# Attention and expert layers in one TensorE stream: how the second group's K reaches its scores, and where two pieces of work are put in the order of issue

## The chip, the core and the metric

The kernel runs on one core of a Trainium2 chip. The metric is the time of one execution in microseconds of the device; lower is better. Engines are named as in the profile: PE (TensorE, matrix products; PEld its weight loads), DVE (VectorE), ACT (ScalarE), POOL (GpSimd), SP (SyncE, which here only issues transfers).

## The reference

Two stages. A linear attention with a complex decay per head and channel, step by step over 768 positions, and a dense layer of four experts on its output.

```python
for t in range(S):                      # S = 768; B, H, D = 4, 8, 48
    new_re = ar * S_re - ai * S_im      # ar, ai: normalised decay of step t
    new_im = ar * S_im + ai * S_re
    S_re, S_im = new_re + einsum('bhd,bhe->bhde', k[:, :, t], v[:, :, t]), new_im
    y[:, :, t] = einsum('bhd,bhde->bhe', q[:, :, t], S_re)
x = y.transpose(0, 2, 1, 3).reshape(3072, 384)
for e in range(4):
    out += p[:, e:e + 1] * (relu(x @ w1[e]) @ w2[e])    # w1[e]: 384 x 1024, w2[e]: 1024 x 384
```

## The kernel before

Products of the expert layers are made in about single precision from parts: each operand is split into a high part and a remainder (hi and lo for weights, xh and xl for x, hh and hl for the hidden values), and three of the four partial products are added up.

The 3072 positions are worked in twelve groups g of 256, counted here from 0, each of two chunks c of 128. For each group three things happen.

**Preparation**, mostly on DVE and ACT. norm scales the decays. prefix forms running products of the decays: steps inside segments of eight (tiles pf), a tree over the segments (sk), and then the four long products and two sums that carry the tree's results to all positions (tile fm; cmul, line 373). finish gives, with q and k, the tiles Q and K: head makes Q, tail makes K. A group's Q and K are laid out by rows of heads, 128 partitions; the scores want them in another layout, 112 partitions by head, in the tiles Qst and Kst.

**Attention** on PE. There are two ways into Qst and Kst. send (line 548) issues ten transfers for one chunk, or for both: five row blocks for the real and five for the imaginary part. With short=True the four blocks of 16 rows are issued from POOL, the other six from SP; otherwise all ten from SP. The other way is over PE: turned (turn0, turn1 for the chunks) transposes K into KT with positions on the partitions (tile ktp), ACT copies it, and turned_back (back0, back1) transposes KT back per head (tile kp, line 601), and ACT copies that to Kst (line 602). KT is needed in any case, by increment (inc0, inc1; tile dp), which forms K times V for the running state Gs. The scores (sc0, sc1; tile sc) multiply Kst with Qst, DVE masks them into scs, values (val0, val1; tile yp) multiplies them with v and adds Qst times the state. ACT copies the result to y. rotate brings the state to the next group's start with the factors of t_factors. Groups 0 and 1 (g < NSEL = 2) go by near_attention, all others by attention. For groups 0 to 2 (g < XSEL = 3), y is turned into x on PE (turn_x, tile xp); from group 3 on, y is stored to memory (y_d) and read back (xa), which all groups store anyway for the second phase. split_x makes xh on ACT and xl on DVE.

**Block** g, the first two experts for the group's x: eight steps of W1 (w1_step, tile ph, 18 products) and W2 (w2_step, tile po, 12 products), W2 one step behind. W1 needs xh of both chunks for its first products, xl for the last three of each half.

The loop over g from 1 on issues block g - 1 (moe1) and, ahead of its step k, calls between(k). There, at step first = FIRST[g] and the steps up to end, one piece of group g's attention is issued (the generator near_attention or attention, cut by its yields), and at the end its x is split. advance issues preparation of the groups to come by planned costs: each yield in norm, prefix and front gives a cost in microseconds, and each step k spends a budget (STEP plus MORE). The scheduler then orders each engine's instructions by a simulated timeline; so what is issued later can run earlier where it is ready. Two helpers bind it: keep_in_program_order keeps an instruction where it was issued, behind(a, b) puts a after b on one engine. wts["w1"] is the first product of the second half of the newest W1 step.

In the second phase, from about 560 us on, the other two experts are worked with a scheme of fewer products; the change doesn't touch it.

For group 1 before the change: Q's first chunk and then its second are sent; K's first chunk goes through turn0 and back0; the third piece (store_y, t_factors, inc1, rotate) is issued at step 7 of block 0.

Of the kernel before, what the change touches and what calls it, by code (L numbers as in the profile page):

```python
# [11 lines left out]
ALU = mybir.AluOpType  # L12
# [23 lines left out]
SEG = 8  # L36
# [21 lines left out]
NSEL = 2  # L58
XSEL = 3
# [66 lines left out]
def fast_path(ctx, tc, qkP, aP, vP, probsP, w, out, flag):  # L126
    nc = tc.nc
# [38 lines left out]
    wts = {}  # L166
# [62 lines left out]
    def split_x(g, parts):  # L229
        xh = moe.tile([P, NJ, G], F32R, tag="xh", name=f"xha{g}")  # L230
        xl = moe.tile([P, NJ, G], F32R, tag="xl", name=f"xla{g}")
        for ts, x in parts:
            ins = nc.scalar.activation(xh[:, :, ts], x, AF.Copy)  # L233
            tc.keep_in_program_order(ins)
            tc.keep_in_program_order(nc.vector.tensor_tensor(xl[:, :, ts], x, xh[:, :, ts], op=ALU.subtract))  # L235
        wts["x"] = ins
        return xh, xl

# [59 lines left out]
    with ExitStack() as c1:  # L298
# [74 lines left out]
        def cmul(x, br, bi, shape, nm):  # L373
            n = 1
            for d in shape:
                n *= d
            names = ["x", "y", "z"][:len(shape)]
            pat = "p c (" + " ".join(names) + ") -> p c " + " ".join(names)
            kw = dict(zip(names, shape))
            half = NJ * G // 2  # L380
            if n <= half:
                t = tmp(f"{nm}a")
                v1, v2 = (t[:, :, k * half:k * half + n].rearrange(pat, **kw) for k in range(2))
            else:
                v1, v2 = (tmp(f"{nm}{k}")[:, :, :n].rearrange(pat, **kw) for k in "ab")
            if len(shape) < 3:
                nc.vector.tensor_tensor(v1, x, bc2(br), op=ALU.mult)
                nc.vector.tensor_tensor(v2, x, bc2(bi), op=ALU.mult)
            else:
                nc.vector.tensor_tensor(v1[:, 0], x[:, 0], br, op=ALU.mult)  # L390
                nc.vector.tensor_tensor(v2[:, 1], x[:, 1], bi, op=ALU.mult)
                nc.vector.tensor_tensor(v1[:, 1], x[:, 1], br, op=ALU.mult)
                nc.vector.tensor_tensor(v2[:, 0], x[:, 0], bi, op=ALU.mult)
            nc.vector.tensor_tensor(x[:, 0], v1[:, 0], v2[:, 1], op=ALU.subtract)
            nc.vector.tensor_tensor(x[:, 1], v1[:, 1], v2[:, 0], op=ALU.add)

        last = {}

# [42 lines left out]
        def prefix(g, A, cuts=(1, NS)):  # L441
            for i in range(1, SEG):
                x = A[:, :, i, :]
                z = tmp(f"pf{g}_{i}").rearrange("p c n -> p (c n)")[:, :4 * MS].rearrange(
                    "p (c d m) -> p c d m", c=2, d=2)
                nc.vector.tensor_tensor(z, x.unsqueeze(2).broadcast_to([P, 2, 2, MS]), bc2(A[:, :, i - 1, :]),  # L446
                                        op=ALU.mult)
                nc.vector.tensor_tensor(x[:, 0], z[:, 0, 0], z[:, 1, 1], op=ALU.subtract)
                nc.vector.tensor_tensor(x[:, 1], z[:, 1, 0], z[:, 0, 1], op=ALU.add)
                yield 1.07  # L450
            Al = A[:, :, SEG - 1, :]
            As = A.rearrange("p c i (j s) -> p c i j s", j=NJ)
            k = 1
            for lo, hi in zip(cuts, cuts[1:]):
                while k < hi:
                    nb = MS // (2 * k)
                    Ak = Al.rearrange("p c (b s) -> p c b s", s=2 * k)
                    br, bi = (Ak[:, c, :, k - 1:k].broadcast_to([P, nb, k]) for c in range(2))
                    cmul(Ak[:, :, :, k:], br, bi, [nb, k], f"sk{g}_{k}")
                    yield 0.9  # L460
                    k *= 2
                shape = [SEG - 1, NJ, hi - lo]
                br, bi = (As[:, c, SEG - 1:, :, lo - 1:hi - 1].broadcast_to([P] + shape) for c in range(2))
                cmul(As[:, :, :SEG - 1, :, lo:hi], br, bi, shape, f"fm{g}_{lo}")
                yield 0

        def pick(g, nm, X, dst, s, w):
# [102 lines left out]
        def chunk(g, c, K, y):  # L570
# [34 lines left out]
            def increment(joined=False):  # L605
                if last:
                    return
                d_ps = ps_a.tile([M, H, D], F32, tag="pa", name=f"dp{g}_{c}")
                for h in range(H):
                    for o, n in ((0, IM), (IM, D)):  # L610
                        ins = nc.tensor.matmul(d_ps[o:o + n, h, :], KT[:, c, h, o:o + n], vc[:, h * D:(h + 1) * D],  # L611
                                               start=True, stop=True)
                        if joined or h or o:
                            tc.keep_in_program_order(ins)
                        if g == 0 and c == 1 and h == 0 and o == 0:
                            behind(ins, wts["w1"])
                Gt = Gs[c]
                if first:
                    nc.scalar.activation(Gt, d_ps, AF.Copy, scale=-1.0)
                else:  # L620
                    nc.vector.tensor_tensor(Gt, state[g, c], d_ps, op=ALU.subtract)
                state[g, c + 1] = Gt
# [89 lines left out]
        def near_attention(g, QK):  # L712
            Q, K = QK
            y = small.tile([M, HP, G], F32, tag="y", name=f"y{g}", bufs=1)
            (turn0, back0, inc0, sc0, val0), (turn1, back1, inc1, sc1, val1) = (chunk(g, c, K, y) for c in range(CG))
            if g == 0:
                turn_over(WARM[1], pick(g, "q", Q, Qst, 0, C))
                yield
                turn0(parts=(0,))
                yield  # L720
                turn_over(WARM[2], turn0(last["act"], parts=(1,)))
                back0()
                state["norm"] = norm(1, A[1], prev=(state["kt", 0, 0], last["dve"], state["kst", 0, 0]))
                next(state["norm"])
                sc0((0,))
                sc0((1,), turn1(prev_pe=state["sc"]))
                inc0()
                yield send(Q, Qst, 1, short=True)
            else:
                yield send(Q, Qst, 0, 1)  # L730
                yield send(Q, Qst, 1)
                turn0()
                back0()
                inc0()
                sc0()
                yield
                turn1()
            back1()
            sc1()
            val0()  # L740
            val1()
            xs = [turn_x(g, c, y) for c in range(CG)]
            yield xs
            store_y(g, y)
            t_factors(g)
            inc1()
            rotate(g)
# [90 lines left out]

        def front(g, A, qk):
            pre = prefix(g, A, cuts if g < NSEL else (1, NS))  # L840
            Q, K, head, tail = finish(g, A, qk)

            def ahead():
                for r in pre:
                    if r == 0:
                        return
                    yield r

            if g < NSEL:
                pieces = near_attention(g, (Q, K))  # L850
                yield from ahead()
                yield 1.8
                head(0, 1)
                yield 1.6
                next(pieces)
                if g == 0:
                    tail(0, 1)
                    next(pieces)
                yield from ahead()
                yield 2.0  # L860
                last["act"] = head(1, CG)
                yield 1.6
                if g > 0:
                    last["q"] = next(pieces)
                    tail(0, 1)
                    yield 2.7
                last["dve"] = tail(1, CG)
                if g == 0:
                    last["q"] = next(pieces)
                yield 2.7  # L870
                todo[g] = pieces
                return
            yield from ahead()
            yield 3.9
            last["act"] = head(0, CG)
            yield 3.0
            yield None
            send(Q, Qst, short=True)
            last["dve"] = tail(0, CG)
            yield 4.8  # L880
            last["q"] = send(K[0], Kst, short=True)
            todo[g] = attention(g, (Q, K))
# [53 lines left out]
        for g in range(1, NG + 1):  # L936
            if g == NG:
                check_all()
            first = FIRST.get(g, 3)
            end = first + (2 if g < NSEL else 1)  # L940

            def between(k, g=g, first=first, end=end):
                if k in LATE.get(g, ()) and NG - 1 in todo:
                    next(late, None)
                if g == 1 and k == 1:
                    for _ in todo.pop(0):
                        pass
                if g == 1 and k > 0:
                    for i in range(NPRE + EARLY + 2 * k - 2, min(NPRE + EARLY + 2 * k, NF1)):
# [594 lines left out]
```

## Time and profile before

| | us |
|---|---|
| median of 3 runs | 960.18 |
| lowest and highest run | 959.71, 960.25 |
| the profiled execution, its own time | 960.0 |
| its span, first to last instruction | 958.2 |
| PE busy in it | 933.9 |
| DVE busy | 745.2 |
| ACT busy | 483.0 |
| POOL busy | 210.7 |

The profile shows one execution. Times in its rows count from the start of the span; busy time is the time in which an engine had an instruction at work. A time in brackets behind an instruction is how long its engine stood idle ahead of it, with what ended that. The granted clock of TensorE is 1.00 of full speed in all the windows read here.

### The profile page before, as it was taken

To read this page: it belongs to the slowest core of one execution; us is meant where nothing else is said; L and a number is where in the kernel's file an instruction comes from. 1 tells how busy PE (TensorE), PEld (TensorE's weight loads), DVE (VectorE), ACT (ScalarE), POOL (GpSimd) and SP (SyncE) were. 2 spreads that over 40 slices of the span, in tenths; PEclk is the share of its full clock that TensorE was granted. 3 is DMA by queue.
4 is the path that set the end of the run, shared out by engine and by line. 5 is a ranking of instruction groups with operands and counts; after the bars stand their busy time and mean duration, and the time that the engine had idled before them with its cause. 6 is when DMAs were issued, how large, how long until landed. Compare 5 with 4: busy or idle time off the path is not lost.

```text
span 958.2 us, 19409 instructions
## 1 busy us (share of the span) xinstructions
PE 933.9 (97%) x7388; PEld 908.3 (95%) x7388; DVE 745.2 (78%) x1630; ACT 483.0 (50%) x1030; POOL 210.7 (22%) x294
## 2 busy tenths in 40 slices
PE   5999999999999999999999999999999999999997
PEld 3899999999999999999999999999999999999997
DVE  7898989989989999888996577748485757666642
ACT  7766446363564736547343555635454554444430
POOL 6030111020211202111111036333424352322000
PEclk9999999999999999999999999999999999999999
DMA  9585264544535546353437799131514433131112
GB/s 314 171 172 139 60 159 89 150 99 142 149 96 129 129 138 156 117 135 109 117 109 226 269 316 275 50 121 38 148 57 144 162 85 102 50 99 51 50 50 78
DMA packets 75029, 125.73 MB, mean 131 GB/s; under 512 B 9600, under 2 KB 50224, under 8 KB 74928
## 3 DMA queue, kind: packets, MB, share of 16 engines
q1 hardware_dynamic: 60464, 94.69, 32.7%
q0 software_dynamic: 14464, 29.72, 13.3%
q8 instruction: 60, 0.98, 0.5%
q14 instruction: 41, 0.34, 0.1%
HBM read 75.94 MB, written 31.46 MB: 112 GB/s over the span
## 4 chain that ended last, share of the span: by engine, by line
PE 89%; DVE 6%; DMA 3%; ACT 2%; issue 1%; SPq 0%; ACTq 0%; DVEq 0%
PE ph L246 21%; PE pob L995 20%; PE po L267 19%; PE pb L995 17%; PE sc L635 3%; PE yp L667 2%; PE dp L611 2%; PE yp L677 2%; PE ktp L584 1%; DMA RX<-w 1%; PE sc L652 1%; DMA shi<-late_d 1%; DVE pf L446 1%; PE xp L706 1%; DVE xl L1001 0%
## 5 line engine op out<-in xcount | busy, mean ns | idle before, releaser
L995 PE MATMUL pob<-shi,hid 128*128 128x384 f32 x528 | 148.5, 335 | 0.5 <-DVE hid L1004 0.5
L267 PE MATMUL po<-whi,hh 128*128 128x384 f32 x384 | 129.7, 338 | 0.0
L267 PE MATMUL po<-wlo,hh 128*128 128x384 f32 x384 | 128.9, 336 | 0.0
L257 ACT ACTIVATE hh<-ph 128x512 fp32r<-128x512 f32 x96 | 57.2, 596 | 121.8 <-PE ph L246 117.5
L1007 POOL TENSOR_TENSOR Z<-Z 128x384 f32<-128x384 f32 x84 | 89.9, 1104 | 114.6 <-DMA Z<-y_d 57.0
L246 PE MATMUL ph<-xha,whi 128*128 128x256 f32 x576 | 103.8, 287 | 1.3 <-ACT xha L233 1.3
L246 PE MATMUL ph<-xla,whi 128*128 128x256 f32 x576 | 101.0, 283 | 2.0 <-DVE xla L235 2.0
L246 PE MATMUL ph<-xha,wlo 128*128 128x256 f32 x576 | 102.0, 284 | 0.0
L995 PE MATMUL pb<-xh,shi 128*128 128x384 f32 x291 | 97.1, 335 | 1.0 <-DVE pb L1001 1.0
L995 PEld LDWEIGHTS pob<-shi,hid 128*128 128x128 f32 x528 | 96.4, 188 | 1.2 <-DVE hid L1004 1.1
L995 PE MATMUL pb<-xl,shi 128*128 128x384 f32 x288 | 96.2, 334 | 0.0
L995 PE MATMUL pb<-xh,slo 128*128 128x384 f32 x288 | 96.2, 334 | 0.0
L246 PEld LDWEIGHTS ph<-xha,whi 128*128 128x128 f32 x576 | 85.9, 190 | 5.3 <-issue 2.4
L258 DVE SCALAR_TENSOR_TENSOR hl<-ph,hh 128x512 fp32r<-128x512 f32 x96 | 65.9, 687 | 31.0 <-ACT hh L257 30.3
L995 PE MATMUL pob<-slo,hid 128*128 128x384 f32 x264 | 88.2, 334 | 0.0
L267 PE MATMUL po<-whi,hl 128*128 128x384 f32 x384 | 85.2, 338 | 0.5 <-DVE hl L258 0.5
L246 PEld LDWEIGHTS ph<-xla,whi 128*128 128x128 f32 x576 | 82.8, 191 | 2.7 <-DVE xla L235 2.4
L246 PEld LDWEIGHTS ph<-xha,wlo 128*128 128x128 f32 x576 | 82.8, 190 | 0.4
L998 ACT ACTIVATE SN<-pb 128x384 f32<-128x384 f32 x96 | 47.4, 494 | 66.7 <-PE pb L995 59.4
L1001 DVE TENSOR_TENSOR xl<-Z,xh 128x384 fp32r<-128x384 f32 x104 | 59.2, 598 | 21.7 <-ACT xh L998 16.3
L998 ACT ACTIVATE hid<-pb 128x384 fp32r<-128x384 f32 x76 | 37.3, 491 | 71.9 <-PE pb L995 71.5
L267 PEld LDWEIGHTS po<-whi,hh 128*128 128x128 f32 x384 | 72.4, 189 | 0.3 <-ACT acc L775 0.2
(238 smaller groups left out, 2119.4 us busy)
## 6 DMA issues: line engine op xcount, KB each, us to landing
qk<-qkP SPq DMA_DIRECT2D x24, 384.0 KB, 4.0
acc_d<-acc POOLq DMA_DIRECT2D x24, 384.0 KB, 5.3
ACC<-acc_d SPq DMA_DIRECT2D x48, 192.0 KB, 3.2
A<-aP SPq DMA_DIRECT2D x22, 384.0 KB, 6.1
v<-vP SPq DMA_DIRECT2D x24, 288.0 KB, 3.0
Z<-y_d SPq DMA_DIRECT2D x16, 384.0 KB, 4.8
Qst<-Q SPq DMA_DIRECT2D x40, 145.1 KB, 3.9
Kst<-K SPq DMA_DIRECT2D x40, 144.0 KB, 3.8
```

What stands on the lines that cost most here:

```text
L246: ins = nc.tensor.matmul(ph[:, u, :], wt[:, j * P:(j + 1) * P], xt[:, j, :], start=(n == 0), stop=(n == 3 * NJ - 1))
L257: wts["hh"] = nc.scalar.activation(hh, ph, AF.Relu)
L258: nc.vector.scalar_tensor_tensor(hl, ph, 0.0, hh, op0=ALU.max, op1=ALU.subtract)
L267: nc.tensor.matmul(po[t], part[0][:, u, t * P:(t + 1) * P], wts[i][n][:, HD:], start=(i % FE == 0 and part[0] is hh and n == 0), stop=(i % ...
L611: ins = nc.tensor.matmul(d_ps[o:o + n, h, :], KT[:, c, h, o:o + n], vc[:, h * D:(h + 1) * D], start=True, stop=True)
L635: ins = nc.tensor.matmul(to, k, q, start=True, stop=True)
L667: ins = nc.tensor.matmul(yo, vc[:, vo:vo + n], scs[2 * c + h // 4][:, h % 4, :], start=True, stop=first)
L677: ins = nc.tensor.matmul(yo, st[:, o:o + n], Qc[:, o // D, :], start=False, stop=True)
L995: return tc.keep_in_program_order(nc.tensor.matmul(*args, **kw))
L998: return pin(nc.scalar.activation(dst, src, fn, scale=scale))
L1001: pin(nc.vector.tensor_tensor(dst, x, y, op=op))
L1007: nc.gpsimd.tensor_tensor(dst, x, y, op=op)
```

## The change

It has three parts.

- Group 1, first chunk of K: sent to Kst by transfers (six on SP, four on POOL) instead of turned back on PE (back0 falls away; turn0 stays for the increment). tail(0, 1), which makes that chunk, is issued ahead of the sends; the second chunk of Q is sent behind K's, and its small blocks are issued from POOL.
- Group 1, the last piece (store_y, t_factors, inc1, rotate): issued at step 1 of block 1, behind its first W1 step, as group 0's already was in block 0, and the increment of chunk 1 is put behind wts["w1"]. The attention's pieces thus take two steps of the block, not three.
- Group 3's prefix: the first long product of fm is put behind the last product of xl of the split issued before it (wts["xl"]), on DVE. cmul returns its first instruction for that.

```diff
--- before.py
+++ after.py
@@ -232,7 +232,8 @@
         for ts, x in parts:
             ins = nc.scalar.activation(xh[:, :, ts], x, AF.Copy)
             tc.keep_in_program_order(ins)
-            tc.keep_in_program_order(nc.vector.tensor_tensor(xl[:, :, ts], x, xh[:, :, ts], op=ALU.subtract))
+            wts["xl"] = nc.vector.tensor_tensor(xl[:, :, ts], x, xh[:, :, ts], op=ALU.subtract)
+            tc.keep_in_program_order(wts["xl"])
         wts["x"] = ins
         return xh, xl
 
@@ -384,15 +385,16 @@
             else:
                 v1, v2 = (tmp(f"{nm}{k}")[:, :, :n].rearrange(pat, **kw) for k in "ab")
             if len(shape) < 3:
-                nc.vector.tensor_tensor(v1, x, bc2(br), op=ALU.mult)
+                ins = nc.vector.tensor_tensor(v1, x, bc2(br), op=ALU.mult)
                 nc.vector.tensor_tensor(v2, x, bc2(bi), op=ALU.mult)
             else:
-                nc.vector.tensor_tensor(v1[:, 0], x[:, 0], br, op=ALU.mult)
+                ins = nc.vector.tensor_tensor(v1[:, 0], x[:, 0], br, op=ALU.mult)
                 nc.vector.tensor_tensor(v2[:, 1], x[:, 1], bi, op=ALU.mult)
                 nc.vector.tensor_tensor(v1[:, 1], x[:, 1], br, op=ALU.mult)
                 nc.vector.tensor_tensor(v2[:, 0], x[:, 0], bi, op=ALU.mult)
             nc.vector.tensor_tensor(x[:, 0], v1[:, 0], v2[:, 1], op=ALU.subtract)
             nc.vector.tensor_tensor(x[:, 1], v1[:, 1], v2[:, 0], op=ALU.add)
+            return ins
 
         last = {}
 
@@ -461,7 +463,9 @@
                     k *= 2
                 shape = [SEG - 1, NJ, hi - lo]
                 br, bi = (As[:, c, SEG - 1:, :, lo - 1:hi - 1].broadcast_to([P] + shape) for c in range(2))
-                cmul(As[:, :, :SEG - 1, :, lo:hi], br, bi, shape, f"fm{g}_{lo}")
+                full = cmul(As[:, :, :SEG - 1, :, lo:hi], br, bi, shape, f"fm{g}_{lo}")
+                if g == XSEL:
+                    behind(full, wts["xl"])
                 yield 0
 
         def pick(g, nm, X, dst, s, w):
@@ -612,7 +616,7 @@
                                                start=True, stop=True)
                         if joined or h or o:
                             tc.keep_in_program_order(ins)
-                        if g == 0 and c == 1 and h == 0 and o == 0:
+                        if g < NSEL and c == 1 and h == 0 and o == 0:
                             behind(ins, wts["w1"])
                 Gt = Gs[c]
                 if first:
@@ -728,9 +732,9 @@
                 yield send(Q, Qst, 1, short=True)
             else:
                 yield send(Q, Qst, 0, 1)
-                yield send(Q, Qst, 1)
+                yield send(K[0], Kst, 0, 1, short=True)
+                yield send(Q, Qst, 1, short=True)
                 turn0()
-                back0()
                 inc0()
                 sc0()
                 yield
@@ -861,8 +865,9 @@
                 last["act"] = head(1, CG)
                 yield 1.6
                 if g > 0:
+                    tail(0, 1)
+                    next(pieces)
                     last["q"] = next(pieces)
-                    tail(0, 1)
                     yield 2.7
                 last["dve"] = tail(1, CG)
                 if g == 0:
@@ -937,13 +942,13 @@
             if g == NG:
                 check_all()
             first = FIRST.get(g, 3)
-            end = first + (2 if g < NSEL else 1)
+            end = first + 1
 
             def between(k, g=g, first=first, end=end):
                 if k in LATE.get(g, ()) and NG - 1 in todo:
                     next(late, None)
-                if g == 1 and k == 1:
-                    for _ in todo.pop(0):
+                if g <= NSEL and k == 1:
+                    for _ in todo.pop(g - 1):
                         pass
                 if g == 1 and k > 0:
                     for i in range(NPRE + EARLY + 2 * k - 2, min(NPRE + EARLY + 2 * k, NF1)):
```

## Rows read from the trace of the kernel before

**Rows 1.** The page, parts 1 and 4: busy time of PE; the chain by engine.
```profile
PE 933.9 (97%) x7388; PEld 908.3 (95%) x7388; DVE 745.2 (78%) x1630; ACT 483.0 (50%) x1030; POOL 210.7 (22%) x294
...
PE 89%; DVE 6%; DMA 3%; ACT 2%; issue 1%; SPq 0%; ACTq 0%; DVEq 0%
```

**Rows 2.** Waits of PE, 60 to 200 us: total, times, longest.
```profile
PE ph L246 <- DVE xla L235: 2.0, 1, 2.0
PE kp L601 <- ACT KT L588: 0.7, 1, 0.7
PE ph L246 <- ACT xha L233: 0.7, 1, 0.7
```

**Rows 3.** Windows: busy time and instructions by engine (PE, PEld, DVE, ACT, POOL), clock, DMA.
```profile
103.00:149.00 46.00, 46.00 (x435) 44.74 (x432) 41.46 (x102) 18.88 (x39) 4.50 (x9) 1.00 0.41 107
...
153.00:195.00 42.00, 41.32 (x405) 39.21 (x405) 38.32 (x86) 21.59 (x47) 4.45 (x9) 1.00 0.48 125
195.00:240.00 45.00, 45.00 (x450) 43.88 (x450) 40.48 (x89) 23.68 (x51) 5.39 (x10) 1.00 0.45 120
```

**Rows 4.** Chain that ended last, in order of time, 84 to 156: start, length, what.
```profile
86.69 0.66 PE kp L601 x6
...
87.58 0.36 PE kp L601 x2
...
88.90 1.98 PE sc L652 x16
...
102.15 1.06 PE dp L611 x30
```

**Rows 5.** Timeline of DVE and ACT, 78 to 90: start, length, instruction.
```profile
78.89 1.02 DVE L543 TENSOR_TENSOR K<-A,u 128x384 f32<-128x384 f32 x2
...
88.05 1.08 ACT L602 ACTIVATE Kst<-kp 112x512 f32<-112x512 f32 x2
```

**Rows 6.** Timeline of SP and POOL: transfers issued, groups 1 and 3.
```profile
88.71 0.83 SPq L367 DMA_DIRECT2D qk<-qkP  x2
...
165.58 3.68 SPq L553 DMA_DIRECT2D Kst<-K  x6
165.84 1.43 POOL L553 DMA_DIRECT2D Kst<-K  x3 [5.44 <-DVE K L543]
...
171.42 0.83 SPq L367 DMA_DIRECT2D qk<-qkP  x2
```

**Rows 7.** DMA issues: count, KB each, median us from issue to landing.
```profile
Kst<-K POOLq DMA_DIRECT2D x40, 16.0 KB, 3.3
...
Qst<-Q SPq DMA_DIRECT2D x8, 72.6 KB, 2.2
...
Qst<-Q SPq DMA_DIRECT2D x4, 72.0 KB, 4.6
```

**Rows 8.** Timeline of ACT, DVE and PE: second halves of two splits; fm and K of group 3.
```profile
102.19 0.49 ACT L233 ACTIVATE xha<-xp 128x384 fp32r<-128x384 f32 x1 [0.85 <-PE xp L706]
...
148.70 0.49 ACT L233 ACTIVATE xha<-xp 128x384 fp32r<-128x384 f32 x1 [2.44 <-PE xp L706]
...
149.34 0.83 DVE L390 TENSOR_TENSOR fm_1a<-A 128x651 f32<-128x651 f32 x1
...
152.93 0.62 PE L246 MATMUL ph<-xla,whi 128*128 128x256 f32 x3 [1.99 <-DVE xla L235]
...
164.60 1.82 DVE L543 TENSOR_TENSOR K<-A,u 128x768 f32<-128x768 f32 x2
```

**Rows 9.** Timeline of PE, start of block 0.
```profile
50.56 0.62 PE L246 MATMUL ph<-xha,whi 128*128 128x256 f32 x3 [0.58 <-ACT xha L233]
```

**Rows 10.** Timeline of PE, first scores of group 3.
```profile
172.52 0.43 PE L635 MATMUL sc<-Qst,Kst 112*64 112x128 f32 x2
```

**Rows 11.** Timeline of ACT and PE, start of block 4.
```profile
238.35 0.85 ACT L233 ACTIVATE xha<-xa 128x768 fp32r<-128x768 f32 x1 [0.53 <-DMA xa<-y_d]
...
239.26 0.61 PE L246 MATMUL ph<-xha,whi 128*128 128x256 f32 x3
```

## The prediction

> **What bounds the kernel now.** I read the page first: TensorE (PE) is busy in 97% of the span, and the chain that ended last is PE in 89% of its length, DVE in 6% [rows 1]. So the end moves by what PE is spared, products or waits, and by little else. The list of PE's waits between 60 and 200 us comes next; three are over half a microsecond, 3.4 us in all [rows 2]. The windows show where PE stands still: not between 103 and 149, 0.68 us between 153 and 195, not after that [rows 3]; the wait for xla falls just after 149 [rows 8]. The same rows show where the danger is: DVE is busy in 41.46 of the 46 us before 149 and in 38.32 of the 42 after 153 (91%). It is a second bound close under PE, and where PE gets ahead, DVE's results may not be there yet.
>
> **First part: K's first chunk by transfers.** Removed in group 1: eight transposes on PE (kp, line 601) and two copies on ScalarE (ACT, line 602). In the chain the transposes alone are 0.66 + 0.36 = 1.02 us; from their first to the scores it is 88.90 - 86.69 = 2.21 us, in which the increment lies too, and undivided that lasts 1.06, so 1.15 at most [rows 4]. I take 1.1. The two copies, 1.08 us of ACT [rows 5], bring nothing beyond it: the scores that waited for them are freed by the transfers instead, and ACT is no bound.
>
> Added: ten transfers of K, six on SP's queue and four on POOL's; four of Q's second chunk go from SP to POOL. DVE has K's first chunk at 78.89 + 1.02 = 79.9, its first half some 0.5 us sooner, at 79.4 [rows 5]. Six such issues take SP 3.68 us in group 3 [rows 6], so the last goes out by 83.1; the large sends of a second chunk, at this place of the group, landed in 2.2 us [rows 7]: K is there at 85.3. On POOL three issues take 1.43 us [rows 6], so four take 1.9, and with 3.3 us to landing [rows 7] it is 79.9 + 5.2 = 85.1. The first scores move from 88.9 to 87.8: 2.5 us of room. The bound from above is the 4.6 us that the large sends of Q's first chunk took under the weights' loads [rows 7]: 87.7, still in time. So no wait. Behind these sends on SP stand the second chunk of Q, and the loads of the next qk and A, which wait for Q's last send and go out at 88.71 [rows 6]. Then: 83.1 + 3.7 = 86.8 for six of Q, plus 2.2, is 89.0, 0.3 us later; A of group 3 and qk of group 2 are read tens of microseconds afterwards. Cost nothing.
>
> The Trainium skill ("DMA: Bandwidth & Descriptors", Rules for kernel authors) speaks against this part: small transfers should be coalesced, and under 64 KB one pays mostly overhead. With that page's fixed 2.0 us and 436 GB/s a send of 72 KB takes an estimated 2.2 us, and the 2.2 of the trace agrees; by rule or by row K lands at 85.3 and the sum is the same, since the overhead lies on queues that are idle here.
>
> The wait of 0.7 us for KT in the same attention [rows 2] belongs to the second chunk, which stays as it is: no gain. Should W2 products of the block come to lie there, 0.7 more is saved; that is the bound from below.
>
> **Second part: last increment behind the next W1.** Store, factors, increment and rotation of group 1 are issued after the first W1 step of block 1. Now the increment fills the 1.06 us between the turning of x and W1 (102.15 to 103.21) [rows 4], while ACT ends the second half of xh at 102.19 + 0.49 = 102.68 [rows 8]. Group 0 shows the place without it: there the increment already lies inside W1, and PE waits 0.58 us for xh [rows 9]. So W1 starts some 0.45 us earlier and pays the 1.06 a little later: a loss of 0.6. From below zero, if W2 products of the last step fill the hole; from above 1.06, if nothing of W1 moves up. The increment's readers on DVE, a difference and four products of the rotation, come later by about 2 us, and who waits for them is the state of group 2, tens of microseconds on; SP's store of y is read in the second phase only. Cost nothing. The 0.5 us of planned budget that goes with the third piece shifts preparation by no more than that.
>
> **Third part: the fourth prefix behind the third x's split.** DVE starts the four long products (fm) of group 3 at 149.34, one every 0.75 us, ahead of the second half of xl of group 2, though ACT has its input ready at 148.70 + 0.49 = 149.19; PE reaches xl, waits 1.99 us and goes on at 152.93 [rows 8]. With the order turned xl runs from about 149.4 to 150.0. PE's products that need only xh last until 152.93 - 1.99 = 150.94, so the wait goes whole: 2.0. DVE pays nothing, for xl lies ahead of fm's closing sums in either order. Bounds: 2.0, or zero if the pin turns out empty because the prefix is issued against an earlier split.
>
> **What is late next.** By now PE is 1.1 - 0.6 + 2.0 = 2.5 us ahead and would reach the scores of group 3, now at 172.52 [rows 10], at 170.0. They read the K that DVE finishes at 164.60 + 1.82 = 166.42 [rows 8], and the load that waits for K's last send goes out at 171.42 [rows 6]: K is in place 1.1 us before it is read now, and 1.4 us too late for a PE that is 2.5 ahead. DVE can gain a little where it waits for PE, and W1 and W2 products can step in while the scores wait; but PE already waits 0.7 us for the x that comes out of this attention [rows 2], so what the scores lose is not all made good. I take 0.5 us back; bounds 0 and 1.4.
>
> **Sum**, against the profiled execution's own 960.0 us (span 958.2): 960.0 - 1.1 + 0.6 - 2.0 + 0.5 = 958.0. That execution is 0.2 us under the median of the runs, 960.18, within their spread. A change of under 0.2%, 1.9 us, can hardly be told from none with this kernel.
>
> **Rivals.**
> 1. DVE and the transfers take most back. K of group 3 does not come earlier, PE's lead shrinks to its 1.1 us of room, and x of group 4 has hardly any room either: ACT ends its xh at 238.35 + 0.85 = 239.20, W1 starts at 239.26 [rows 11]. Time 960.0 - 1.1 = 958.9, between 958.3 and 960.2. For it: DVE's 91%. Against: DVE has 4.5 idle us of 45 after 195 [rows 3], enough to catch up. The case of an empty pin ends here too: 960.0 - 1.1 + 0.6 = 959.5.
> 2. Slower: K's first chunk lands late. PE runs in the order written, so scores that stand ahead of their K stop all behind them, one for one from 87.8 on. It decides from 90.3, where the 2.5 us are eaten up; from 92.2 on the kernel is 0.2% slower. Landing at 92.7 would give 960.0 + 0.6 - 2.0 + 4.9 - 1.1 = 962.4. For it: 4.6 us to landing under load, and ten sends in place of eight transposes. Against: even those 4.6 end at 87.7, and no wait of PE for a K that was sent stands in its list. The rule of the Trainium skill on small transfers, named above, would point this way.
> 3. Better: W2 products fill the 0.7 us of the attention's wait and the hole of 0.6, and K of group 3 keeps up: 960.0 - 1.1 - 0.7 - 2.0 = 956.2.
>
> **Chances.** The forecast, with its own range of 957.0 to 958.26: 0.42. Better: 0.12. DVE takes it back: 0.34. Slower: 0.12, a sixth of it with a loss under 0.2%. Faster by over 0.2% (under 958.26) is then 0.54, within 0.2% 0.36, slower 0.10. The range of 956.2 to 961.0 leaves out the far end of the better case and most of the slower one.
>
> **What would show it.** Right: no kp products in group 1, its first scores about 1.1 us earlier and without a wait for Kst; PE waiting about 0.6 us for xha ahead of block 1; no wait for xla at block 2; the scores of group 3 near 170.5. Wrong: a wait of PE for sent K near 88 us; a wait for xha ahead of block 3 that has grown from 0.7 us by what was saved before; waits at later blocks, where there are none now.

## The result, and the profile after

The changed kernel is slower: 965.91 us in the median of 6 runs (964.48 to 967.23), against 960.21 (959.47 to 961.91, 6 runs) for the kernel before on the same chip. The ratio is 1.0059, with a 95% interval of 1.0046 to 1.0072. The profiled execution took 966.38 us with a span of 964.7, 6.5 us more than the span before.

All three edits are to be seen where they were meant to act. The loss comes behind them. The third part binds only the product that cmul returns, so one of the four long products still runs ahead of xl (149.00), then xl (149.76), then the other three; that is enough to take PE's wait away. First, PE's waits between 60 and 200 us in the changed kernel (total, times, longest; [rows 2] is the same list before):

```profile
PE ph L247 <- ACT xha L233: 4.0, 2, 3.4
PE kp L605 <- ACT KT L592: 1.2, 1, 1.2
```

The wait of 2.0 us for xla is gone. The wait for xha, one of 0.7 before, is now two: 0.58 ahead of block 1 and 3.40 ahead of block 3. The wait for KT has grown by half a microsecond. Between 200 and 560 us, where the kernel before waits for nothing that its list names, there are two more:

```profile
PE sc L639 <- DMA Kst<-K: 0.9, 1, 0.9
PE po L268 <- ACT acc L779: 0.9, 1, 0.9
```

The windows of the changed kernel show the same by place (length, then busy time of PE, PEld, DVE, ACT and POOL with their instructions, granted clock, DMA share, GB/s):

```profile
0.00:60.00 60.00, 46.62 (x377) 38.57 (x378) 48.83 (x130) 43.19 (x89) 23.67 (x42) 1.00 0.73 223
60.00:103.00 43.00, 40.95 (x356) 39.41 (x355) 38.82 (x101) 24.47 (x53) 11.03 (x19) 1.00 0.72 167
...
149.00:153.00 4.00, 4.00 (x34) 4.00 (x33) 3.97 (x7) 1.48 (x3) 0.91 (x1) 1.00 0.14 16
...
194.00:196.00 2.00, 0.00 (x0) 0.00 (x0) 1.06 (x2) 0.00 (x0) 0.00 (x0) 1.00 0.55 185
196.00:198.00 2.00, 1.05 (x5) 1.05 (x6) 1.07 (x2) 0.84 (x1) 0.00 (x0) 0.77 0.00 0
198.00:200.00 2.00, 2.00 (x9) 2.00 (x9) 1.39 (x2) 0.49 (x2) 0.00 (x0) 0.50 0.00 0
...
200.00:300.00 100.00, 98.26 (x923) 95.56 (x922) 87.87 (x187) 53.98 (x108) 15.52 (x29) 1.00 0.50 123
```

Four of the same windows of the kernel before:

```profile
0.00:60.00 60.00, 47.58 (x377) 39.01 (x378) 48.73 (x130) 43.39 (x89) 23.65 (x42) 1.00 0.73 223
60.00:103.00 43.00, 42.06 (x392) 40.62 (x390) 38.56 (x101) 25.44 (x55) 7.07 (x11) 1.00 0.68 157
...
149.00:153.00 4.00, 2.02 (x16) 1.61 (x14) 3.97 (x9) 1.25 (x3) 0.91 (x1) 1.00 0.29 35
...
200.00:300.00 100.00, 99.98 (x937) 97.25 (x936) 90.22 (x190) 51.85 (x105) 15.02 (x28) 1.00 0.52 135
```

From 153 to 200, PE was busy for 46.32 us and now is for 43.60. So the idle time of PE grows by 1.1 us between 60 and 103, falls by 2.0 at block 2, grows by 2.7 around block 3 and by 1.7 between 200 and 300. The first 60 us, which no edit touches, add 1.0 in this execution; in the profiled executions of the other kernels, which don't touch them either, they hold 46.6 to 47.6, so this is chance. Besides, PE's own busy time grows, from 933.9 to 935.3 us, with eight transposes fewer: behind the long wait the granted clock stands at 0.50, half speed, and the first products of block 3 take 0.92 and 0.84 us instead of 0.62 and 0.52. These sums come to 5.9 of the 6.5 us; the rest is spread over the time after 300.

Where the long wait comes from is read on PE's timeline. SPq is SP's queue of transfers. These are the products that stand just ahead of group 3's scores in the changed kernel, and x's way to block 3:

```profile
171.39 0.34 PE L268 MATMUL po<-whi,hh 128*128 128x384 f32 x1
...
172.44 0.34 PE L268 MATMUL po<-wlo,hh 128*128 128x384 f32 x1
172.71 0.43 PE L639 MATMUL sc<-Qst,Kst 112*64 112x128 f32 x2
...
187.70 0.95 SPq L756 DMA_DIRECT2D y_d<-y  x2
...
192.73 0.39 SPq L226 DMA_DIRECT2D xa<-y_d  x1
196.06 0.84 ACT L233 ACTIVATE xha<-xa 128x768 fp32r<-128x768 f32 x1 [5.34 <-DMA xa<-y_d]
196.95 0.92 PE L247 MATMUL ph<-xha,whi 128*128 128x256 f32 x3 [3.40 <-ACT xha L233]
```

The way of x in the kernel before:

```profile
186.95 0.95 SPq L752 DMA_DIRECT2D y_d<-y  x2
190.77 0.39 SPq L226 DMA_DIRECT2D xa<-y_d  x1
194.02 0.84 ACT L233 ACTIVATE xha<-xa 128x768 fp32r<-128x768 f32 x1 [4.90 <-DMA xa<-y_d]
194.91 0.62 PE L246 MATMUL ph<-xha,whi 128*128 128x256 f32 x3 [0.68 <-ACT xha L233]
```

K was ready in time: DVE ends it at 165.74 (166.42 before, [rows 8]), and the load that waits for its sends goes out at 170.15 (171.42 before, [rows 6]). Yet the scores start at 172.71, 0.2 us later than before [rows 10]. PE comes to block 2 at 149.51 instead of 149.25 and no longer waits there, so it works 23.2 us from there to the scores, where it worked 21.3. The 1.9 us are products that the plan now places ahead of the scores: W1 of step 5 whole (before, nine of its 18), and seven of the twelve of W2's step 4 (before, none). Inside the attention it is the same: the first increment begins when it did (178.61, and 178.58 before), but eight products of W2 in place of four lie between it and the second chunk's values, which begin 0.75 us later (185.00 instead of 184.25), and with them y's store. What lies ahead of the attention no longer lies behind it, where the kernel before used it to cover x's way through memory. PE runs out of work at 193.55, 0.7 us sooner than before, and x comes 2.0 us later.

### The profile page after: what moved, and what is told of

The parts are those of the page before. It is cut to its first block, busy times and chain, and to the rows that moved or that the text cites. A ratio compares the mean times of both kernels' runs of the same rounds, so it can differ in the third digit from the quotient of the medians.

```text
span 964.7 us, 19406 instructions
## 1 busy us (share of the span) xinstructions
PE 935.3 (97%) x7380; PEld 909.4 (94%) x7380; DVE 746.2 (77%) x1630; ACT 481.1 (50%) x1028; POOL 214.6 (22%) x302
## 4 chain that ended last, share of the span: by engine, by line
PE 84%; DVE 7%; DMA 4%; ACT 4%; issue 1%; SPq 0%; ACTq 0%; DVEq 0%
PE pob L1000 20%; PE ph L247 19%; PE po L268 17%; PE pb L1000 16%; PE sc L639 3%; PE yp L671 2%; PE dp L615 2%; PE yp L681 2%; PE ktp L588 1%; PE xp L710 1%; PE sc L656 1%; DMA late_d<-lwl 1%; DVE xl L1006 1%; DMA Z<-y_d 1%; DMA late_d<-lwm 1%
```

## The experiments

**The parts one by one.** The third part's binding is called the pin in what follows. Four kernels: the third part alone, the first alone, the second alone, and both without the third. Each leaves the other parts of the diff out. The third part alone is this, with cmul returning its first product:

```diff
+            wts["xl"] = nc.vector.tensor_tensor(xl[:, :, ts], x, xh[:, :, ts], op=ALU.subtract)
...
+                full = cmul(As[:, :, :SEG - 1, :, lo:hi], br, bi, shape, f"fm{g}_{lo}")
+                if g == XSEL:
+                    behind(full, wts["xl"])
```

> The kernel before with the third part alone (first long product of group 3's prefix behind the third x's split). Theory A, order of issue: the pin changes PE's planned order in block 2, the scores of group 3 stand behind more W1 and W2 products, fewer products are left behind its attention to cover the way of x through memory, PE stalls about 3 us ahead of block 3. Then this alone costs most of the loss: 963 to 966 us. Theory B, the transfers of K and the late last piece are the loss: this alone saves the 2.0 us wait, 958 us. Theory C, the loss needs all parts together because PE's lead adds up: 959 to 961 us.

Measured: 966.0 us (5 runs, 965.65 to 966.58), ratio 1.0055 (1.0041 to 1.0069). The wait ahead of block 3 is 3.43 us, and the clock behind it 0.50.

The first part alone:

```diff
-                yield send(Q, Qst, 1)
+                yield send(K[0], Kst, 0, 1, short=True)
+                yield send(Q, Qst, 1, short=True)
                 turn0()
-                back0()
```

> The kernel before with the first part alone (first chunk of K of group 1 by transfers, eight transposes fewer). Theory A: PE's order in block 2 is as before, so at most the 1.1 us of transposes are saved, less what the wait for KT takes: 959 to 960.3 us. Theory B: slower by 2 us or more, 962 us or above. Theory C: 959 to 961 us.

Measured: 961.29 us (11 runs), ratio 1.0006 (0.9997 to 1.0015). The profiled execution, 961.89 us, has a stretch of half speed behind the wait at block 2, of which the last section tells.

The second part alone:

```diff
-            end = first + (2 if g < NSEL else 1)
+            end = first + 1
...
-                if g == 1 and k == 1:
-                    for _ in todo.pop(0):
+                if g <= NSEL and k == 1:
+                    for _ in todo.pop(g - 1):
```

> The kernel before with the second part alone (last piece of group 1 behind the first W1 step of block 1). Theory A: a loss of 0.6 us for the hole ahead of block 1, some of it swallowed by slack before block 2: 960.2 to 961 us. Theory B: slower by 2 us or more. Theory C: 959 to 961 us.

Measured: 959.94 us (11 runs), ratio 0.9992 (0.9983 to 1.0001). PE is later here at block 2, and its wait for xla there is 1.5 us instead of 2.0: most of what the second part loses comes back in that wait.

The first and second part, so the diff without the lines shown for the third:

> The changed kernel without its third part (first and second part together). Theory A: within 1 us of the kernel before, 959.3 to 961 us, with no wait over 1 us ahead of block 3 and a granted clock of 1.00 there. Theory B: like the changed kernel, 964 to 967 us. Theory C: 959 to 961 us, as each part alone.

Measured: 960.78 us (11 runs), ratio 1.0000 (0.9991 to 1.0009). The kernel before stood at 960.74 beside these four. So the pin, an order between two products on DVE, brings the whole loss by itself, and the other two parts are worth nothing that can be measured in the old order.

**Is the low clock a cost of the wait?** In the changed kernel, 19 products that nothing reads fill the place where PE waits for x.

```diff
+                if b == 3 and f2 == 0:
+                    prev = wts["w1e"]
+                    ps = wts["ps_a"].tile([P, HD], F32, tag="pa", name=f"fill{b}")
+                    for _ in range(19):
+                        ins = nc.tensor.matmul(ps, wts[0][0][:, :P], wts[0][0][:, :HD], start=True, stop=True)
+                        behind(ins, prev)
+                        prev = ins
                 hh, hl = w1_step(b, xh, xl, f2, prev if f2 == f_lo // 2 else None)
```

> The changed kernel, with 19 products of 128 x 384 that nothing reads, put on TensorE into the place where it waits 3.4 us for the x of group 3, ahead of block 3. They change no order and bring x no earlier. They take about 3.1 us of the 3.4, so a wait of about 0.3 us should be left. If the granted clock of 0.50 behind that wait is a cost of the wait (products of 0.92 and 0.84 us where they take 0.62 and 0.52), the clock stays at 1.00 and the time falls by 1.2 to 1.6 us, to 964.3 to 964.7. If the low clock has nothing to do with the wait, the time stays at 965.9; if the products themselves delay the block, it is above that.

Measured: 970.04 us (5 runs; before 961.63), ratio 1.0093 (1.008 to 1.0106), which no expectation had. The timeline shows both halves of the answer. The added products (fill) run ahead of the last products of W2, and no wait is left ahead of block 3:

```profile
192.01 3.45 PE L290 MATMUL fill<-whi 128*128 128x384 f32 x19
...
196.69 0.59 PE L247 MATMUL ph<-xha,whi 128*128 128x256 f32 x3
...
201.40 0.52 PE L247 MATMUL ph<-xla,whi 128*128 128x256 f32 x3
...
203.89 1.07 ACT L258 ACTIVATE hh<-ph 128x512 fp32r<-128x512 f32 x2
204.53 0.44 PE L268 MATMUL po<-whi,hh 128*128 128x384 f32 x1 [2.60 <-ACT hh L258]
```

In the changed kernel:

```profile
202.40 0.60 ACT L258 ACTIVATE hh<-ph 128x512 fp32r<-128x512 f32 x1 [0.37 <-PE ph L247]
...
203.22 0.52 PE L247 MATMUL ph<-xla,whi 128*128 128x256 f32 x3
```

The clock stays at 1.00. The same 40 products, the first two steps of W1 with four of W2, take 4.7 us from the start of the first to the start of the last three (196.69 to 201.40), where they took 6.3 (196.95 to 203.22). So the half speed cost some 1.6 us. But then PE waits 2.6 us for hh. There ACT made the first hh of block 3 at 202.40, and PE went on without a wait. Here ACT's order is another: eight operations of preparation, from 198.38 on, stand ahead of it, and it comes at 203.89. Later waits follow, up to 560 us: 1.9 for copies of po and 0.7 for xla, where the changed kernel has 0.9 for a copy of po and 0.9 for K. Nineteen products on one engine changed the order on another, and that took more than the clock gave.

**Is it PE's lead that does the harm?** The third part alone, with 11 such products ahead of block 2, in the place of the removed wait.

```diff
+                if b == 2 and f2 == 0:
...
+                    for _ in range(11):
```

> The third part alone, with 11 products of 128 x 384 that nothing reads ahead of block 2: they take about 1.8 us, the place of the wait for xla that this part removes, so TensorE has no lead over the kernel before. Theory A (the wait is only moved: the order that is planned for a TensorE ahead of K spends the lead on W products in front of the attention and has none left behind it) expects about 960.5, since the scores stand 19 products behind the turning again, three fewer than now, and more is left behind the attention: the 2 us are paid in the products and not at block 3. If the pin hurts by itself (DVE's work in another order, K or x of group 3 later), the time stays at 964 or more, and the wait ahead of block 3 stays at 2 us or more.

Measured: 967.16 us (5 runs), ratio 1.0065 (1.0052 to 1.0078). The theory's 960.5 fell. The wait ahead of block 3 is 1.39 us, not 3.4, and the clock stays at 1.00; but PE now waits for hh (0.9), for the copies of po (1.6 in two) and for xla (0.7) between 200 and 560 us. Giving PE the time back does not give the old order back. So this run can't tell what the old order would take with PE's lead gone.

**Does the order on PE do it?** The changed kernel, with W2 of step 4 and W1 of step 6 of block 2 put behind group 3's scores, so that the products that had moved ahead come behind (sc3 is the last product of these scores).

```diff
+                if g == XSEL:
+                    wts["sc3"] = ins
...
+                if b == 2 and f2 == 6:
+                    prev = wts["sc3"]
+                hh, hl = w1_step(b, xh, xl, f2, prev if f2 == f_lo // 2 or b == 2 and f2 == 6 else None)
...
-                    w2_step(f2, hh, hl, po)
+                    w2_step(f2, hh, hl, po, wts["sc3"] if b == 2 and f2 == 4 else None)
```

> The changed kernel, with W2 of step 4 and W1 of step 6 of block 2 put behind the scores of group 3, so that the products that the plan had put in front of the scores come behind them (about 10 of them, some 1.8 us). K is in place at 170.2. Theory A expects the scores at about 171.5 instead of 172.7, x of group 3 some 1.5 us sooner, a wait ahead of block 3 under 1.5 us instead of 3.4, no low clock behind it, and a time of about 962. If the cause is elsewhere (a slow store of y, a late DVE), x comes no sooner and the time stays at 965.9.

Measured: 961.39 us (12 runs; before 961.63), ratio 1.0000 (0.9992 to 1.0009). Rows of PE and SP and two windows of this kernel:

```profile
171.49 2.91 PE L643 MATMUL sc<-Qst,Kst 112*64 112x128 f32 x64
...
185.50 0.94 SPq L762 DMA_DIRECT2D y_d<-y  x2
189.58 0.39 SPq L226 DMA_DIRECT2D xa<-y_d  x1
```

```profile
194.00:200.00 6.00, 6.00 (x48) 6.00 (x47) 5.09 (x11) 4.39 (x9) 0.89 (x1) 1.00 0.46 66
...
240.00:260.00 20.00, 17.88 (x142) 17.17 (x143) 16.18 (x25) 11.75 (x25) 4.80 (x9) 1.00 0.57 117
```

The scores start 1.2 us sooner than in the changed kernel, y's store goes out 2.2 us sooner and the load of x 3.2, and no wait is left ahead of block 3. So of the 3.2 us, 1.2 are the scores' place; 1.0 is gained inside the attention and 0.9 on the store's way, and no run parts these from the scores. With one order on PE the whole loss is made good. But there is no gain either: PE, by now some 2 us ahead of the kernel before, stands still for 2.1 us in block 4.

**What holds block 4?** This is the same kernel there, on ACT, DVE and PE:

```profile
248.53 0.94 ACT L425 ACTIVATE u<-s,lnb 128x768 f32<-128x768 f32 x1 [2.50 <-DMA Qst<-Q]
...
250.38 0.96 DVE L434 TENSOR_TENSOR u<-s,u 128x768 f32<-128x768 f32 x1 [2.21 <-ACT u L433]
251.25 1.82 DVE L551 TENSOR_TENSOR K<-A,u 128x768 f32<-128x768 f32 x2
...
258.25 0.40 PE L643 MATMUL sc<-Qst,Kst 112*64 112x128 f32 x2 [1.26 <-DMA Kst<-K]
```

ACT's norm of group 6 waits for the sends of Q; DVE stands 2.2 us behind it, and K of group 5 is queued behind that product. In the kernel before the same two were the other way round:

```profile
248.48 1.82 DVE L543 TENSOR_TENSOR K<-A,u 128x768 f32<-128x768 f32 x2
250.22 0.95 DVE L428 TENSOR_TENSOR u<-s,u 128x768 f32<-128x768 f32 x1
```

The changed kernel has the swap too, with 1.84 us of DVE's waiting. So it was undone, by itself and together with the scores' order; state["K", 5] is the last product of that K.

```diff
+                    ins = nc.vector.tensor_tensor(v, m2, v, op=ALU.mult)
+                    if g == 6 and n == 0:
+                        behind(ins, state["K", 5])
```

> The changed kernel, with nothing changed but that the first product of group 6's norm is put behind the K of group 5 on VectorE. It measures the second place of the loss by itself: a wait of 0.9 us of TensorE for the sends of that K. Theory A expects 965.0, and the wait of 3.4 us ahead of block 3 with its low clock unchanged. If this wait only stands for a VectorE that is behind anyway, the time stays at 965.9.

Measured: 965.37 us (6 runs, 963.12 to 967.0; before 961.35), ratio 1.0046 (1.0031 to 1.006). No wait for Kst is left in its list, and the wait ahead of block 3 is 2.96 us. The step from 1.0059 to 1.0046 has about the size that was expected, 0.9 us, but the intervals overlap, and a part of it may be the clock, which stayed at 1.00 behind the wait in this kernel's profiled execution.

> The changed kernel with the scores of group 3 kept early, as in scores_kept_early (961.39 us), and one more order: on VectorE, the first product of group 6's norm behind the K of group 5, as it was before. In the changed kernel that product stands ahead of K and waits 1.8 us for ScalarE; in scores_kept_early it waits 2.2 us, K of group 5 is begun at 251.25 instead of 248.48, and TensorE waits 1.3 us for its sends. Theory A expects this wait to go: 961.4 - 1.3 = 960.1, and 959.2 if the wait of 0.9 us for the copy of po in the same block goes too. If VectorE simply has too much work for a TensorE that is 2 us ahead, the wait comes back a group later and the time stays at 961.4.

Measured: 959.74 us (11 runs, 959.17 to 961.34; before 961.35 in 23 runs), ratio 0.9988 (0.9979 to 0.9997). In block 4:

```profile
248.12 1.83 DVE L553 TENSOR_TENSOR K<-A,u 128x768 f32<-128x768 f32 x2
250.37 0.96 DVE L434 TENSOR_TENSOR u<-s,u 128x768 f32<-128x768 f32 x1 [0.42 <-ACT u L433]
...
256.10 0.43 PE L645 MATMUL sc<-Qst,Kst 112*64 112x128 f32 x2
```

K starts 3.1 us sooner than in the kernel above, and the scores 2.2. This is the best version of the study and the only one whose interval lies below the kernel before: by 0.12%, some 1.2 us in the median.

**Are the first two parts worth something in the mended order?** The third part alone, with both orders.

> The third part alone, with both orders of scores_and_k_early. The first two parts measured 1.0006 and 0.9992 alone, so the time should be that of scores_and_k_early to within 0.5 us: 959.7 to 960.6. If the first two parts are worth what the prediction gave them together (0.5 us saved), it is 0.5 above; if they are worth a gain only where the third part's order is mended, it is further above.

Measured: 961.62 us (11 runs), ratio 1.0006 (0.9997 to 1.0015), 1.9 us above the kernel with all three parts. Three rows of this kernel:

```profile
164.37 1.82 DVE L553 TENSOR_TENSOR K<-A,u 128x768 f32<-128x768 f32 x2
171.99 3.18 PE L645 MATMUL sc<-Qst,Kst 112*64 112x128 f32 x64 [0.34 <-DMA Kst<-K]
...
195.18 0.63 PE L247 MATMUL ph<-xha,whi 128*128 128x256 f32 x3 [0.76 <-ACT xha L233]
```

K of group 3 starts at 164.37 instead of 163.95, PE waits 0.34 us for it and 0.76 for x ahead of block 3, where the kernel with all three parts has neither wait, and y's store goes out at 186.25 instead of 185.50. Much later, at 429, PE waits 0.39 us for another K. So the first two parts seem to help once K is what PE waits for; how they make K earlier was not followed further.

**The store of y.** In the changed kernel x's way took 1.2 us longer between the last issue of y's store (188.65) and the load of x (192.73, 4.1 us) than before (187.90 to 190.77, 2.9). A load of v goes out 0.84 us ahead of the store (186.86 and 187.70). The kernel before has the same load as far ahead (186.11 and 186.95), so it could hardly make the difference. The changed kernel, with that load behind the store (state["store", g] is the last issue of y's store of group g):

```diff
+            ins = nc.sync.dma_start(vc, vP[g * G + c * C:g * G + (c + 1) * C, :])
+            if g == XSEL + 1:
+                behind(ins, state["store", g - 1])
```

> The changed kernel, with the loads of group 4's v issued behind the store of group 3's y on SyncE. The store took 4.3 us to land, against 3.1 before, and a load of v went out 0.85 us ahead of it. If that load holds the store up, y lands about 1.2 us sooner, the wait ahead of block 3 is 2.2 us, and the time is about 964.5. If the store is slow for another reason, nothing moves: 965.9.

Measured: 967.36 us (6 runs; before 961.63), ratio 1.0059 (1.0045 to 1.0073). The store still takes 3.9 us to the load of x (issues end at 188.67, the load goes out at 192.56), and the wait is 3.07 us. That the load stands ahead of the store is not the cause:

```profile
187.73 0.94 SPq L758 DMA_DIRECT2D y_d<-y  x2
188.77 1.35 SPq L580 DMA_DIRECT2D v<-vP  x2
192.56 0.39 SPq L226 DMA_DIRECT2D xa<-y_d  x1
```

Both loads of v now go out right behind the store, so the run doesn't exclude that transfers in flight beside it make it slow. The time of this kernel says less than its rows: its half speed lasts longer than in the changed kernel, and PE is busy for 938.0 us instead of 935.3.

## Why the prediction was wrong

The forecast was 958.0 us, the median 965.91. The prediction named the sign that would prove it wrong: a wait for xha ahead of block 3 that has grown by what was saved before. That is the largest of the new waits. The last sign that it named, waits at later blocks, came too.

**First part, forecast 1.1 saved: mis-sized.** No transpose of the first chunk is left, and its scores start at 86.16 instead of 88.83, without a wait for the K that was sent; rival 2 did not happen. (The prediction's estimate of 2.2 us for a send uses the fixed 2.0 us and 436 GB/s that the Trainium skill gives, in "DMA: Bandwidth & Descriptors", Anatomy of one DMA, for transfers issued from GpSimd. The large sends go out from SP, so the row with 2.2 us [rows 7] decides.) Most of those 2.7 us is work that only moved behind the first scores: the increment and four W2 products. The wait for KT at the second chunk grew from 0.68 to 1.22, since ACT still had a norm and the copies of po to do:

```profile
91.95 1.09 PE L605 MATMUL kp<-wide,KT 128*112 128x128 f32 x8 [1.22 <-ACT KT L592]
93.28 2.05 PE L656 MATMUL sc<-Qst,Kst 112*128 112x128 f32 x16 [0.25 <-ACT Kst L606]
```

The second chunk's scores start at 93.28 instead of 93.56. So the term was 0.3, not 1.1; and alone the part measured 1.0006. The prediction had counted the 0.7 us as a wait that stays or shrinks, while here it grew by 0.54 us, half of the 1.0 that the eight transposes had taken.

**Second part, forecast 0.6 lost: the mechanism and the size were right.** PE waits 0.58 us for xha ahead of block 1, the increment lies at 105.52 inside W1, and W2 of block 1 starts at 108.12 instead of 107.55. In the time of the whole kernel it doesn't show (0.9992 alone), since with this part alone the wait for xla behind it shrinks from 2.0 to 1.5 us.

**Third part, forecast 2.0 saved: right where it was made.** xla is done at 150.31 instead of 152.88, PE's wait is gone, and W2 of block 2 starts at 153.81 instead of 155.91.

**The step that failed is "What is late next".** It let PE reach group 3's scores at 170.0 with the products in their old order, found K 1.4 us late there, and put 0.5 us back, 1.4 at most. The runs showed three things in its place. First, the order is not kept: the scheduler writes a new order for a PE that is 2 us ahead, and puts W products in front of the scores, though their K is in place by 170.15 and read at 172.71. The lead is spent in front of the attention instead of being kept behind it. Second, the x of group 3 does not merely fail to come earlier; it comes 2.0 us later, 0.75 of it with y, behind four more W2 products, and 1.2 in the store's way to memory, whose cause is open. With the 0.7 by which PE runs out of work sooner this makes the 2.7 us by which the wait at block 3 grew, and the half speed behind it cost some 1.6 more. Third, the same happens on DVE two groups on: a product of a norm ahead of K, and 0.9 us of PE. The bound of 1.4 us would hold only for an order that stays.

That the order of issue is the cause is shown from both sides: the pin on DVE alone makes the loss (1.0055), and one order on PE, with the pin left in, takes it away (1.0000). How much of it goes by the scores' place alone is not shown, since each binding makes the scheduler write the rest anew as well. Whether PE's lead would do harm in the old order stays open too: with the lead given back in products the time was 967.16, but in yet another order. Of rival 1, which saw DVE's results too late for a faster PE, half is true: in the mended kernel K of group 5 is what comes late. It is late because of its place in DVE's queue, not because DVE had too much to do, for with the place mended the wait is gone and the time is 959.74.

Open remain the 1.2 us of the store, and the 0.9 us of waiting for the copy of po in block 4, which the best kernel still has.

## What to carry to other kernels

Where a scheduler orders the instructions by a simulated timeline, a wait that is removed is not yet time that is saved: the orders behind it can be written anew. Read the order on all engines after the change, ahead of the next input that comes from memory above all, and hold it with a few bindings; here two of them turned a loss of 0.6% into a gain of 0.1%. And when PE gets ahead, look at each wait that it already has behind that place: a wait for another engine can take back some of the lead, as the one for KT did (0.68 to 1.22 us), and a product that waits holds up what stands behind it on its engine, as the norm's product held up K (2.21 us).

## What the runs showed of the hardware

- Around the end of a wait of PE the granted clock fell, in some executions, to 0.50, the lower of its two levels (1.2 of 2.4 GHz): so in the changed kernel with 3.40 us of waiting, in the third part alone with 3.43, and with the loads of v moved with 3.07, where it was 0.50 in all of 196 to 202. With 2.96 us, in the kernel with K's order alone, it stayed at 1.00. In the first part alone the wait of 2.0 us at block 2 was followed by a clock of 0.76 in the mean from 153 to 160, with 0.50 from 155 to 157, where the kernel before, with the same wait, has 1.00. So the length of the wait did not decide by itself in these executions, of which each kernel has one. With the long wait filled the clock stayed at 1.00. Here is the window from 198 to 200 at either level:

```profile
198.00:200.00 2.00, 2.00 (x9) 2.00 (x9) 1.53 (x3) 0.83 (x2) 0.00 (x0) 0.50 0.00 0
```

```profile
198.00:200.00 2.00, 2.00 (x19) 2.00 (x18) 0.96 (x2) 1.92 (x4) 0.16 (x1) 1.00 0.00 0
```

  The first is the third part alone: PE busy throughout and nine products. The second is K's order alone, with 19 in the same time. The runs go with it: the changed kernel took 964.48 us at a mean clock of 0.999 and 967.23 at 0.996, and the kernel with K's order alone 963.12 at 0.999 and 967.00 at 0.994.
- The same store of y, 192 KB in each of two issues, took from 2.5 to 4.2 us from the end of its issues to the load that waits for it, and from 3.6 to 5.2 from the start of its first issue, in kernels that differ only in order. No run shows why.
